# Products over 448 rows: six 128-row matmuls and a pair of 64-row halves, or seven pairs of 64-row halves

## The chip, the core and the metric

The kernel runs on one NeuronCore of a Trainium2 chip. The core has five engines with instruction streams of their own: PE (TensorE, matmuls), DVE (VectorE), ACT (ScalarE), POOL (GpSimd) and SP (SyncE, which here only issues DMAs). They meet through semaphores. The metric is the device time of one execution in microseconds (us), median of several runs; less is better.

## What is computed

x is 2048 x 448 in bf16. It is normalised row by row, and two branches are added to it: a linear attention with 16 heads of 28 columns, and a feed-forward layer with 1792 hidden columns. Cut to what matters:

```python
xn = _layernorm(x)                                    # 2048 x 448
q, k, v = split(xn @ wqkv)                            # 16 heads, Dh = 28
pq, pk = q @ w_phi, k @ w_phi                         # per head, 28 x 28
phi_q = concat(softmax(pq), softmax(-pq)); phi_k = concat(softmax(pk), softmax(-pk))
kv, z = phi_k^T v, sum(phi_k)
o = (phi_q kv) / (phi_q z + 1e-6)
h = xn @ w1 + b1;  act = h * tanh(softplus(h))        # Mish, F = 1792
out = x + o @ wo + act @ w2
```

## The kernel before

The 2048 tokens are 16 tiles of 128, taken as 8 pairs `u`, the two tiles of a pair being `par` 0 and 1. The weights of w_phi are first multiplied into those of q and k (steps `wtk`, `wmk`, `wmq`), so q, k and v are one product each. All products with 448 rows of contraction share one layout: 448 = 3 x 128 + 64. Each pair has a transposed copy `xnT[:, u]` of seven 128-row chunks: three for `par` 0, three for `par` 1, and one shared chunk whose upper 64 rows are the last 64 of `par` 0 and whose lower 64 rows are those of `par` 1 (`xchunk`).

Such a product is two steps on PE. Part **F** has six matmuls over all 128 rows, three for each `par`. Part **H** has two matmuls over 64 rows, one in the upper half of the array for `par` 0 and one in the lower half for `par` 1. Both parts of one product add into a pair of neighbouring PSUM banks, one bank for each `par`; `take2` and `free2` keep four such pairs. The part that comes second closes the sum, and ACT or DVE reads it. `pair_part` (its matmuls are line 426) does this for `v{u}`, `k{u}`, `q{u}` (448 columns, 8 pairs each) and for `f{q}.{fc}`, the first feed-forward layer (512 columns, 28 products). `wo` (line 831) does it for the output projection, whose bank also takes the second layer `g{t}` (`ffn2`, line 815, 14 matmuls over 128 rows each). `finish` (line 780) adds x and a store follows.

Three other groups of matmuls are not changed: `kv{u}` (line 641, two column halves of the array side by side), `nd{t}` (line 715, 16 small matmuls in the two 64-row halves, 60 columns each) and the transposes and weight products at the start (lines 499, 550, 574). `z12` (line 371) are twelve matmuls on zeros ahead of all others.

The order of everything is written out by hand in `ORDER`: a list of step names, each of which appends instructions to the streams of its engines. Each engine works its own stream strictly in that order; `Program.op` finds which earlier operations of other engines an operation must wait for, `resolve` drops the waits that are implied, `emit` writes them. Operations on the same PSUM bank by the same engine need no wait in this scheme. SP's stream holds nearly all DMAs: loads (`l...s`), transposes by DMA of the normalised rows (`xt{u}m`, line 511), of the query features (`e{t}`, line 681), of the attention output (`ot{u}m`, line 749), and stores (`sto`, `stt`). Steps named later: `pw`, `zero`, `pv`, `pm`, `pi` are POOL's first memsets and masks; `qd` (line 284) completes the transposed q weights on DVE, which `wmq0` and `wmq1` on PE (line 574) read; `st{u}` are row statistics on DVE; `l1ms` loads three quarters of w1 (line 271), `l2s` w2, `los` wo.

Of the kernel before, what the change touches and what calls it, by code (L numbers as in the profile page):

```python
# [38 lines left out]
class Program:  # L39
# [113 lines left out]
e9 f0.2H kn2.0 e13 f0.2F kn7.0 f0.0F f1.2F f0.1F f0.0H f0.1H f1.3H q5H kn1.0 f1.3F kn0.1 e8 q0F q0H f0.3H kn0.0 q7H  # L153
kn3.1 e5 e1 q5F q7F f0.3F f1.7F kv7 kn1.1 kv0 kv4 kv6 kv3 kv2 kv1 e0 kv5 e10 f1.1H kvz f1.7H f1.8H f1.1F f1.8F f0.6F
e14 e11 f1.5H f0.6H nd2 f0.10F f1.5F nd1 f0.10H f0.5H f0.5F f1.11F nd3 ot1m f1.11H nd0 f0.13H f0.13F e15 f1.12F f1.0F
f1.0H ot0m f1.12H los wob nd6 f1.13F f0.7F f1.10H f0.7H nd7 l2s ot3m f1.13H f1.10F f0.4F f0.4H nd5 f0.12H f0.9H f0.9F
f0.12F nd4 f0.11H f0.8H f0.8F f0.11F f1.4F f1.6H f1.4H nd10 ot2m f1.9H f1.9F f1.6F wo3F wo3H nd11 nd13 nd12 ot5m ot6m
# [10 lines left out]
def _kernel(es, nc, A_x, A_wqkv, A_w_phi, A_wo, B_w1, B_b1, B_w2, out):  # L168
# [218 lines left out]
    def take2(hold=True):  # L387
        free = [b for b in (0, 2, 4, 6) if b not in held]
        assert free, "no pair of banks"
        b = min(free, key=lambda b: max(used[b], used[b + 1]))  # L390
        touch(b, b + 1)
        if hold:
            held.add(b)
        return b
# [7 lines left out]
        touch(b)  # L402
        return b

    def pe(fn, r, w, tag):
        return op("PE", fn, r=r, w=w, tag=tag)

    open_ = {}

    def pair_part(key, part, works, r, then):
        if key not in open_:
            open_[key] = take2()
            first = True
        else:
            first = False
        b = open_[key]  # L420

        def f(e):
            for o, par, lhs, rhs in works(b):
                for c in range(3) if part == "F" else (3,):
                    k = (0, P) if part == "F" else HALF[par]
                    ins = e.matmul(o, lhs(c, k), rhs(c, k), start=first and c in (0, 3), stop=not first and c in (2, 3))  # L426
            return ins
# [168 lines left out]
        return c if c == 3 or par == 0 else 4 + c  # L596

    def tok_works(u, W):
        return lambda b: [(bank(b + par)[:, 0:D], par,
                           lambda c, k, par=par: xnT[k[0]:k[1], u, xchunk(c, par), :],  # L600
                           lambda c, k: W[k[0]:k[1], c, :]) for par in range(2)]

# [59 lines left out]


    def feat_works(W, cols, q, rows):
        return lambda b: [(bank(b + par)[0:rows, :], par,
                           lambda c, k: W[k[0]:k[1], c, cols],
                           lambda c, k, par=par: xnT[k[0]:k[1], 4 * q:4 * q + 4, xchunk(c, par), :])
                          for par in range(2)]
# [95 lines left out]
        return CUT if t == LAST else D  # L764

    out_bank = {}
    done = {t: 0 for t in range(NT)}

    def out_part(t):

        u = t // 2
        if u not in out_bank:
            out_bank[u] = take2()
        done[t] += 1
        return out_bank[u] + t % 2, done[t] == 1, done[t] == 3

    def finish(t):
        b = out_bank[t // 2] + t % 2
        n = width(t)
        op("DVE", lambda e: e.tensor_tensor(x_all[:, t, 0:n], bank(b)[:, 0:n], x_all[:, t, 0:n], ALU.add),  # L780
           r=[pb(b), ("x", t)], w=[("out", t)], tag=f"fin{t}")
        if t == LAST:
            last_columns(t, b ^ 1)
        if done[t] == done[t ^ 1] == 3:
            free2(out_bank[t // 2])

    def last_columns(t, b):
        assert done[t ^ 1] == 3
# [12 lines left out]
        op("DVE", lambda e: e.tensor_tensor(x_all[:, t, CUT:D], to, x_all[:, t, CUT:D], ALU.add), r=[pb(b), ("x", t)],  # L801
           w=[("outl", t)], tag=f"finl{t}")
# [18 lines left out]

    def wo(u, part):
        places = [out_part(2 * u + par) for par in range(2)]

        def f(e):
            for par, (b, first, last) in enumerate(places):
                for c in range(3) if part == "F" else (3,):
                    lo, hi = (0, P) if part == "F" else HALF[par]
                    cc = xchunk(c, par)
                    n = width(2 * u + par)  # L830
                    ins = e.matmul(bank(b)[:, 0:n], oT_of(u)[lo:hi, cc * P:(cc + 1) * P], Wo[lo:hi, cc, 0:n],  # L831
                                   start=first and c in (0, 3), stop=last and c in (2, 3))
            return ins
        pe(f, [("oT", u)] + [("Wo", n) for n in range(4)], [pb(b) for b, _, _ in places], f"wo{u}{part}")
        for par, (b, first, last) in enumerate(places):
            if last:
                finish(2 * u + par)
# [15 lines left out]
    for u in range(NU):  # L853
# [8 lines left out]
            add(f"xt{u}{c}", xT, u, eng)  # L862
            add(f"ot{u}{c}", oT, u, eng)
        for eng, c in (("ACT", "a"), ("DVE", "d")):
            for part in "FH":
                add(f"v{u}{part}{c}", v_mm, u, part, eng)
        for part in "FH":
# [15 lines left out]
            for which, n in ((0, "q"), (1, "k")):  # L883
                add(f"wm{n}{h}{c}", w_mm, which, h, eng)
    for q in range(2):
        for part in "FH":
            for fc in range(FC):
                add(f"f{q}.{fc}{part}", ffn1, q, fc, part)
    add("kvz", kvz)
# [75 lines left out]
```

## Time and profile before

| | |
|---|---|
| time, median of 3 runs | 153.92 us (153.82 to 154.27) |
| profiled execution: span from first to last instruction | 151.8 us |
| PE busy / weight loads busy | 147.1 us (97%), 1181 matmuls / 72.7 us (48%) |
| DVE / ACT / POOL busy | 101.2 us / 75.2 us / 40.0 us |
| granted TensorE clock, mean | 0.998 |
| DMA traffic | 17.17 MB, mean 113 GB/s |

The profile gives one execution. Its span runs from the first to the last instruction; the time of a run is taken from outside and holds 2.1 us more (153.92 - 151.8). In the timeline a row gives start, duration, engine, line, operation, out<-in, the size of the part of the array used (rows*columns), the shape and a count; consecutive instructions of one kind are merged, so a row of `x8` may hold six 128-row matmuls and two 64-row ones, under the shape of the first. Because matmuls are pipelined, their durations overlap: the distance from one start to the next tells what PE gives to each, the duration tells when its result is there. `PEld` are the weight loads, one for each matmul. Square brackets give idle time ahead of the row and what ended it; "issue" means nothing that the profile shows.

### The profile page before, as it was taken

The page shows a single profiled execution, that of the slowest core. Times are in us where ns is not written, and L with a number is a line of the kernel's source. Part 1 is how long each engine was busy: PE and PEld are TensorE (multiplying, and loading weights), DVE is VectorE, ACT ScalarE, POOL GpSimd, SP SyncE. Part 2 cuts the span into 40 slices and gives each one's busy share as a digit, 9 for nine tenths or more (in the row PEclk, how much of TensorE's full clock was granted, in tenths as well). Part 3 has the DMA queues.
Part 4 walks back from the last instruction along what each step waited for, and adds up shares of the span by engine and source line. Part 5 has one row for each costly group of instructions (what it writes and reads, how often), then busy time and mean ns, then how long its engine had stood idle before and what let it go on. Part 6 is the DMA issues. An engine that isn't in the chain of part 4 may idle for free.

```text
span 151.8 us, 2885 instructions
## 1 busy us (share of the span) xinstructions
PE 147.1 (97%) x1181; PEld 72.7 (48%) x1181; DVE 101.2 (67%) x227; ACT 75.2 (50%) x91; POOL 40.0 (26%) x58
## 2 busy tenths in 40 slices
PE   7799999999999999999999999999999999999993
PEld 2365444454444475444444444655555555455552
DVE  0699997999999203298999847798795970311221
ACT  4988999898998996756558567000000000000000
POOL 7452562499999950000000000000000000000000
PEclk9999999999999999999999999999999999999999
DMA  5994995989767091910389950030207021110302
GB/s 135 253 269 84 292 163 103 185 255 231 159 139 139 0 176 41 170 36 0 73 157 317 319 81 10 0 67 18 43 0 213 33 39 21 60 35 0 121 0 91
DMA packets 39961, 17.17 MB, mean 113 GB/s; under 512 B 33932, under 2 KB 39180, under 8 KB 39948
## 3 DMA queue, kind: packets, MB, share of 16 engines
q1 hardware_dynamic: 39776, 16.89, 50.0%
q8 instruction: 9, 0.15, 0.4%
q10 hardware_dynamic: 172, 0.10, 0.2%
q14 instruction: 4, 0.03, 0.1%
HBM read 7.02 MB, written 1.84 MB: 58 GB/s over the span
## 4 chain that ended last, share of the span: by engine, by line
PE 92%; ACT 2%; DMA 2%; DVE 1%; issue 1%
PE PS L426 51%; PE PS L815 28%; PE PS L831 7%; PE PS L715 3%; PE PS L641 2%; DMA x_all<-in_A_x_dram 2%; PE PS L574 1%; ACT junk L447 1%; DVE xn L491 1%; ACT junk L452 1%; PE PS L499 0%; DVE x_all L780 0%; ACT rmean L450 0%; ACT lnv L470 0%; ACT rstd L472 0%
## 5 line engine op out<-in xcount | busy, mean ns | idle before, releaser
L426 PE MATMUL PS<-xnT,W 128*128 128x512 bf16 (+1 forms) x224 | 46.3, 380 | 0.0
L815 PE MATMUL PS<-W,actT 128*128 128x448 bf16 (+1 forms) x224 | 42.8, 351 | 0.0
L692 ACT ACTIVATE actT<-PS,b1T 128x1024 bf16<-128x1024 f32 x28 | 30.5, 1113 | 13.7 <-PE PS L426 13.6
L815 PEld LDWEIGHTS PS<-W,actT 128*128 128x128 bf16 x224 | 21.8, 98 | 20.2 <-issue 0.4
L426 PEld LDWEIGHTS PS<-xnT,W 128*128 128x128 bf16 (+1 forms) x224 | 17.6, 97 | 23.8 <-issue 5.3
L624 POOL TENSOR_TENSOR actT<-actT,rSk 128x896 bf16<-128x896 bf16 x16 | 26.6, 1700 | 4.4 <-DVE rSk L622 4.4
L780 DVE TENSOR_TENSOR x_all<-PS,x_all 128x448 bf16<-128x448 f32 (+1 forms) x16 | 9.6, 617 | 20.9 <-PE PS L815 17.7
L620 DVE TENSOR_REDUCE Sk<-actT 128x32 f32<-128x896 bf16 x16 | 16.7, 1041 | 0.9 <-ACT actT L612 0.9
L612 ACT ACTIVATE actT<-PS 128x896 bf16<-128x896 f32 x16 | 13.7, 940 | 0.4 <-PE PS L426 0.4
L426 PE MATMUL PS<-Wpq,xnT 128*128 128x448 bf16 (+1 forms) x64 | 12.9, 352 | 0.0
L426 PE MATMUL PS<-Wpk,xnT 128*128 128x448 bf16 (+1 forms) x64 | 12.7, 353 | 0.0
L426 PE MATMUL PS<-Wkv,xnT 128*128 128x448 bf16 (+1 forms) x64 | 12.6, 353 | 0.0
L730 DVE COPY Sq<-PS 128x16 f32<-128x16 f32 x32 | 4.0, 167 | 10.8 <-PE PS L715 10.8
L456 DVE BATCH_NORM_STATS2 stats<-x_all 128x6 f32<-128x448 bf16 x14 | 8.5, 605 | 3.4 <-DMA x_all<-in_A_x_dram 3.4
L738 DVE TENSOR_TENSOR v_all<-v_all 128x464 f32<-128x464 f32 x16 | 10.3, 642 | 0.6
L734 DVE TENSOR_TENSOR v_all<-PS,Sq 128x464 f32<-128x464 f32 x16 | 10.3, 641 | 0.5
L741 DVE TENSOR_TENSOR xn<-v_all,rden 128x448 bf16<-128x448 f32 x16 | 10.0, 625 | 0.6
L736 DVE TENSOR_TENSOR v_all<-PS,Sq 128x464 f32<-128x464 f32 x16 | 10.1, 629 | 0.0
L673 ACT ACTIVATE actT<-PS 128x896 bf16<-128x896 f32 x10 | 8.5, 932 | 0.1
L426 PEld LDWEIGHTS PS<-Wpk,xnT 128*128 128x128 bf16 (+1 forms) x64 | 5.3, 97 | 6.1 <-issue 1.9
L426 PEld LDWEIGHTS PS<-Wpq,xnT 128*128 128x128 bf16 (+1 forms) x64 | 5.3, 97 | 5.7 <-issue 1.1
L426 PEld LDWEIGHTS PS<-Wkv,xnT 128*128 128x128 bf16 (+1 forms) x64 | 5.1, 97 | 5.7 <-issue 1.5
(86 smaller groups left out, 117.4 us busy)
## 6 DMA issues: line engine op xcount, KB each, us to landing
W<-in_B_w_dram SPq DMA_DIRECT2D x1, 1568.0 KB, 8.3
out_dram<-x_all SPq DMA_DIRECT2D x7, 224.0 KB, 2.2
W<-in_B_w_dram SPq DMA_DIRECT2D x1, 1344.0 KB, 7.1
x_all<-in_A_x_dram SPq DMA_DIRECT2D x4, 224.0 KB, 3.1
x_all<-in_A_x_dram SPq DMA_DIRECT2D x2, 448.0 KB, 4.8
Wkv<-in_A_wqkv_dram SPq DMA_DIRECT2D x2, 336.0 KB, 4.7
Wo<-in_A_wo_dram SPq DMA_DIRECT2D x2, 336.0 KB, 3.8
W<-in_B_w_dram SPq DMA_DIRECT2D x2, 224.0 KB, 4.4
```

The source lines that it names most:

```text
L426: ins = e.matmul(o, lhs(c, k), rhs(c, k), start=first and c in (0, 3), stop=not first and c in (2, 3))
L612: op("ACT", lambda e, s=s: e.activation(E_of(u)[:, s, :, :], two(b, D), ACT.Exp, scale=1.0 if s == 0 else -1.0), r=[pb(b), pb(b + 1)], w=[ ...
L620: op("DVE", lambda e: e.tensor_reduce(Sk[u][:, s, :], Eh(), AX.X, ALU.add), r=[("E", u, s)], w=[("Sk", u, s)], tag=f"Sk{u}.{s}")
L624: op("POOL", lambda e: e.tensor_tensor(Eh(), Eh(), ap_on(rSk[u][:, s, 0:1], [[1, 2 * H], [0, DH]]), ALU.mult), r=[("E", u, s), ("rSk", u, ...
L692: op("ACT", lambda e: e.activation(actT[:, fc, q * 1024:(q + 1) * 1024], bank(b, 2), ACT.Mish, bias=b1T[:, fc:fc + 1]), r=[("b1T",), pb(b) ...
L734: op("DVE", lambda e: e.tensor_tensor(tv(t1[i]), num(0), sx(1), ALU.mult), r=[pb(b), pb(b + 1), ("Sq", i, 1)], w=[("t1", i)], tag=f"ta{t}")
L736: op("DVE", lambda e: e.tensor_tensor(tv(t2), num(1), sx(0), ALU.mult), r=[pb(b), pb(b + 1), ("Sq", i, 0)], w=[("t2",)], tag=f"tb{t}")
L738: op("DVE", lambda e: e.tensor_tensor(t1[i], t1[i], t2, ALU.add), r=[("t1", i), ("t2",)], w=[("t1", i)], tag=f"tc{t}")
L741: op("DVE", lambda e: e.tensor_tensor(o_sb[(t // 2) % 2][:, t % 2, :].rearrange("p (h d) -> p h d", d=DH), t1[i][:, :, 0:DH], ap_on(rden[i ...
L780: op("DVE", lambda e: e.tensor_tensor(x_all[:, t, 0:n], bank(b)[:, 0:n], x_all[:, t, 0:n], ALU.add), r=[pb(b), ("x", t)], w=[("out", t)], ...
L815: ins = e.matmul(bank(b)[:, 0:width(t)], actT[:, fc, tok(t)], W2[:, fc, 0:width(t)], start=first and fc == 0, stop=last and fc == FC - 1)
L831: ins = e.matmul(bank(b)[:, 0:n], oT_of(u)[lo:hi, cc * P:(cc + 1) * P], Wo[lo:hi, cc, 0:n], start=first and c in (0, 3), stop=last and c i ...
```

## The change

Each product over 448 rows may now be cut in three parts instead of two. **A** has the three 128-row chunks of each `par` in their halves: for each chunk, the upper 64 rows of `par` 0 in the upper half of the array and the lower 64 rows of `par` 1 in the lower half, six matmuls in three pairs. **B** has the other halves, crossed over: lower rows of `par` 0, upper rows of `par` 1, again six in three pairs. **H** is as before. So a product has 14 matmuls in 7 pairs, not 8 (6 and a pair). In A and H the upper half of the array writes the bank of `par` 0, in B that of `par` 1. Where two steps on the same pair of banks differ in this, the second gets a wait on PE's own semaphore for the first (`side`, `after`). Part F remains possible, but the new `ORDER` uses A, B and H everywhere: 1541 matmuls instead of 1181, and 68 waits of PE on its own semaphore instead of none. `ORDER` is new throughout; its steps are the same but for the parts. The diff, cut to what matters:

```diff
-    def op(self, eng, fn, r=(), w=(), dma=False, tag=""):
+    def op(self, eng, fn, r=(), w=(), dma=False, tag="", after=()):
...
-        deps = []
+        deps = list(after)
...
-table lx2s lba zero lx3s pv st2b pw lkms lps pi pm st3b rs3a lkts z12 b1 pp rs2p lx1s xn2d xn3d wtk0b xt2b wtk1b lvms
-lx4s lqT2 st1 bd pk lqT0 xt3a wmk0b lqT1 rs1a wmk1a xn1d st5 rs5p v2Fd lqT3 v3Fa v3Ha k2H v2Ha k3H qd xt1m lx0s st4
-k2F rs4p wmq0d xn4d xn5p wmq1a k3F v1Fd st0 q3F k1H q3H lx6s st6 v1Hd q2H q2F rs6p st7 k1F q1F l1ts rs0p xt4m xt5m
-xn6d k4F rs7p k4H e6 v5Hd xn0d xt6m xn7d kn4.1 q1H k5H xt0m v5Fd k5F kn5.0 v6Fd kn5.1 k6F k0H xt7m ep e7 v6Ha k7H
-l1ms k6H k7F kn6.0 k0F kn6.1 e3 q6F e2 v0Fa kn2.1 kn7.1 v4Fd v0Ha v4Hd kn4.0 q6H v7Hd kn3.0 v7Fa q4F e4 e12 f1.2H q4H
...
+table lx2s pw lba zero pv pm st2b lx3s lkms lps st3b lkts z12 pi rs2p rs3a lx1s b1 xn2d wtk0b lvms lx4s xn3d xt2b
+wtk1b bd wmk0b st1 xt3a v2Ad st5 wmk1a pk lqT2 v3Ha lqT0 rs1a lqT1 v2Ha v3Aa lqT3 pp v2Bd qd xn1d k2H v3Ba lx0s k2A
+rs5p wmq0d wmq1a k2B k3A k3H q2B st4 rs4p k3B lx6s xt1m xn5p q3A q2A q2H st7 k1B rs7p st6 l1ts q3B xt5m xn4d rs6p xn7d
+kn3.0 q1B q3H k1A xt4m xt7m v1Bd k1H q1A v1Ad xn6d k5B v1Hd q1H k5A k5H st0 v5Hd rs0p v5Ad kn1.0 xt6m k4B v5Bd k7A
+l1ms kn5.0 k4A v7Hd k4H k7H v7Aa k7B v6Ad xn0d v7Ba k6H kn5.1 v6Ha k6A v6Bd e3 kn2.0 kn7.1 xt0m q4B k6B e2 v4Bd q4A
+q4H kn1.1 v4Hd v4Ad k0A kn6.0 kn3.1 v0Ba k0B e7 v0Aa e6 k0H v0Ha q6H q6A f1.2B q6B f0.0H f1.2A f0.2B kn2.1 f1.2H e4
...
+    open_ = {}
+    side = {}
+
+    def passes(part):
+        if part == "F":
+            return [(c, par, (0, P)) for par in range(2) for c in range(3)]
+        x = int(part == "B")
+        return [(c, r ^ x, HALF[r]) for c in ((3,) if part == "H" else range(3)) for r in range(2)]
+
+    def pe_pass(fn, r, b, part, tag):
+        o = pe(fn, r, [pb(b), pb(b + 1)], tag, after=[side[b, "A" if part == "B" else "B"]] if part in "ABH" and
+               (b, "A" if part == "B" else "B") in side else [])
+        side[b, "B" if part == "B" else "A"] = o
+
+    def run(e, todo, works, first, last):
+        at = {par: [n for n, x in enumerate(todo) if x[1] == par] for par in range(2)}
+        for n, (c, par, k) in enumerate(todo):
+            o, lhs, rhs = works[par]
+            ins = e.matmul(o, lhs(c, k), rhs(c, k), start=first and n == at[par][0], stop=last and n == at[par][-1])
+        return ins
...
     def pair_part(key, part, works, r, then):
+        todo = passes(part)
         if key not in open_:
-            open_[key] = take2()
...
-        pe(f, r, [pb(b), pb(b + 1)], key + part)
-        if not first:
+            open_[key] = [take2(), set()]
+        b, done = open_[key]
+        first = not done
+        done.add(part)
+        last = done in ({"F", "H"}, {"A", "B", "H"})
+        pe_pass(lambda e: run(e, todo, works(b), first, last), r, b, part, key + part)
+        if last:
             then(b)
             free2(b)
```

`wo` is changed in the same way (it calls `passes` and `pe_pass`), and `finish` counts four parts instead of three for each output tile. In the new `ORDER` the steps `kv` stand in one block as before, the `nd` steps stand among the products, and the `g` steps stand in three blocks and at the end.

More of the change, by code (lines that the diff above doesn't have):

```diff
@@ L153 @@
[L153 to L157, printed above, removed]
@@ new lines @@
+f1.6A f0.12H f0.9B los e10 f1.11H f1.6H e15 e14 f0.9A f0.13B f0.9H l2s f0.13A f0.13H f1.13A nd0 f1.11B f1.13H f1.11A
+f0.6A f1.13B f0.6B nd3 f1.7A f0.6H f1.7H f0.4B f1.7B nd2 f0.4H f0.4A e1 f0.7B f0.5H f0.7H ot1m f0.7A f1.10A f0.5A
+f1.4B nd7 f0.5B f1.10B f1.4H f1.10H f1.4A f0.3B nd1 f0.3H f0.11H f0.11A f1.8H f0.3A f1.5A f0.11B f1.5B f1.8B ot0m
+f1.5H f0.10B nd5 f1.8A f0.10H f0.10A f0.8B f1.9B nd4 f0.8A f0.8H f1.9H f1.9A wo1B ot2m nd6 wo1H ot3m nd13 wo1A nd12 g2
+g0 g3 g1 nd11 ot6m f1.12B f1.0A f1.12H f1.0B wo0H wo0A f1.0H wo0B wo2A wo2H sto0 f1.12A wo6H nd9 sto1 wo6A wo2B wo6B
@@ L160 @@
+nd10 nd8 ot4m g5 g12 ot5m g4 g11 g9 g10 g13 wo4H nd14 wo4B wo3A wo5H wo3H wo5A nd15 ot7m wo3B g6 sto6 g7 g8 sto3 wob
+wo5B wo7B wo4A wo7A sto2 wo7H sto5 g14 sto4 g15 stt14 stt15
 """
@@ L403, in take1, with pe @@
         return b
-    def pe(fn, r, w, tag):
-        return op("PE", fn, r=r, w=w, tag=tag)
+    def pe(fn, r, w, tag, after=()):
+        return op("PE", fn, r=r, w=w, tag=tag, after=after)
     open_ = {}
+    side = {}
[14 more added lines that the diff above has]
+        return ins
     def pair_part(key, part, works, r, then):
+        todo = passes(part)
         if key not in open_:
-            open_[key] = take2()
[L417 to L427, printed above, removed]
-        pe(f, r, [pb(b), pb(b + 1)], key + part)
-        if not first:
+            open_[key] = [take2(), set()]
[5 more added lines that the diff above has]
+        if last:
             then(b)
@@ L598, in tok_works @@
     def tok_works(u, W):
-        return lambda b: [(bank(b + par)[:, 0:D], par,
+        return lambda b: [(bank(b + par)[:, 0:D],
                            lambda c, k, par=par: xnT[k[0]:k[1], u, xchunk(c, par), :],
@@ L664, in feat_works @@
     def feat_works(W, cols, q, rows):
-        return lambda b: [(bank(b + par)[0:rows, :], par,
+        return lambda b: [(bank(b + par)[0:rows, :],
                            lambda c, k: W[k[0]:k[1], c, cols],
@@ L766, in _kernel, with parts_of @@
     out_bank = {}
+    STEPS = ORDER.split()
+    def parts_of(t):
+        return 3 if f"wo{t // 2}F" in STEPS else 4
     done = {t: 0 for t in range(NT)}
@@ L774, in out_part @@
         done[t] += 1
-        return out_bank[u] + t % 2, done[t] == 1, done[t] == 3
+        return out_bank[u] + t % 2, done[t] == 1, done[t] == parts_of(t)
     def finish(t):
@@ L783, in finish @@
             last_columns(t, b ^ 1)
-        if done[t] == done[t ^ 1] == 3:
+        if done[t] == done[t ^ 1] == parts_of(t):
             free2(out_bank[t // 2])
     def last_columns(t, b):
-        assert done[t ^ 1] == 3
+        assert done[t ^ 1] == parts_of(t)
         to = bank(b)[:, D:D + 64]
@@ L823, in wo @@
         places = [out_part(2 * u + par) for par in range(2)]
+        todo = passes(part)
         def f(e):
[L826 to L832, printed above, removed]
+            at = {par: [n for n, x in enumerate(todo) if x[1] == par] for par in range(2)}
+            for n, (c, par, (lo, hi)) in enumerate(todo):
+                b, first, last = places[par]
+                cc = xchunk(c, par)
+                w = width(2 * u + par)
+                ins = e.matmul(bank(b)[:, 0:w], oT_of(u)[lo:hi, cc * P:(cc + 1) * P], Wo[lo:hi, cc, 0:w],
+                               start=first and n == at[par][0], stop=last and n == at[par][-1])
             return ins
-        pe(f, [("oT", u)] + [("Wo", n) for n in range(4)], [pb(b) for b, _, _ in places], f"wo{u}{part}")
+        pe_pass(f, [("oT", u)] + [("Wo", n) for n in range(4)], places[0][0], part, f"wo{u}{part}")
         for par, (b, first, last) in enumerate(places):
@@ L864, in _kernel @@
         for eng, c in (("ACT", "a"), ("DVE", "d")):
-            for part in "FH":
+            for part in "FABH":
                 add(f"v{u}{part}{c}", v_mm, u, part, eng)
-        for part in "FH":
+        for part in "FABH":
             add(f"k{u}{part}", k_mm, u, part)
@@ L885, in _kernel @@
     for q in range(2):
-        for part in "FH":
+        for part in "FABH":
             for fc in range(FC):
```

4 lines of the change are left out of this document (2 added, 2 removed).

## Prediction

> **What bounds the kernel now.** I read the page's busy table first, then the slices and the chain that ended last, then the table of waits.
>
> ```profile
> PE 147.1 (97%) x1181; PEld 72.7 (48%) x1181; DVE 101.2 (67%) x227; ACT 75.2 (50%) x91; POOL 40.0 (26%) x58
> ...
> PE   7799999999999999999999999999999999999993
> ...
> PEclk9999999999999999999999999999999999999999
> ...
> PE 92%; ACT 2%; DMA 2%; DVE 1%; issue 1%
> ```
> ```profile
> PEld PS L426 <- issue: 9.8, 26, 0.4
> ```
>
> PE is busy in every slice after the first and carries 92% of the chain, at the full clock. It waits for almost nobody, so time can only come from what PE does between its matmuls, or be lost by making PE wait. The waits row shows where to look: the weight loads of the products stood still 26 times, about 0.4 us each, for no releaser. The PE timeline shows what these places are.
>
> ```profile
> 22.91 1.59 PE L426 MATMUL PS<-Wpk,xnT 128*128 128x448 bf16 x8
> 24.34 0.35 PE L426 MATMUL PS<-Wkv,xnT 64*128 64x448 bf16 x2
> 24.53 0.35 PE L426 MATMUL PS<-Wpq,xnT 64*128 64x448 bf16 x2
> 24.72 0.35 PE L426 MATMUL PS<-Wpk,xnT 64*128 64x448 bf16 x2
> 25.00 1.31 PE L426 MATMUL PS<-Wkv,xnT 128*128 128x448 bf16 x6
> 26.15 1.30 PE L426 MATMUL PS<-Wpk,xnT 128*128 128x448 bf16 x6
> 27.29 1.30 PE L426 MATMUL PS<-Wkv,xnT 128*128 128x448 bf16 x6
> 28.42 1.59 PE L426 MATMUL PS<-Wpk,xnT 128*128 128x448 bf16 x8
> ```
>
> Twelve 128-row matmuls start from 26.15 to 28.42: 0.189 us each. A pair of 64-row halves follows the one before it after 0.19 (24.34, 24.53, 24.72). So two halves side by side cost what one full matmul costs, and the 14 matmuls of the new product in 7 pairs cost what 6 and a pair cost now. The changes between the two shapes cost extra. From 22.91 to 24.34 lie six full matmuls and a pair, 7 x 0.189 = 1.32, and it took 1.43: 0.11 to go in. From 24.72 to 25.00 lies one pair, 0.28 for 0.19: 0.09 to come out.
>
> **The change, part by part.** *Changes of shape.* Counted along PE's stream, before goes 20 times from 128-row matmuls into 64-row ones and 21 times back; `nd` counts as 64-row. After, it does this 6 and 6 times (the start's weight products, four blocks of `g`), and once more comes out into `kv`, which before was entered from full matmuls. That removes 14 x 0.11 + 15 x 0.09 = **2.9 us** of PE time, nothing of which lay beside another wait of PE. I take the same price for the 512-column products.
>
> The Trainium skill, "TensorEngine Tiling (Array Packing)", Key Properties, says that changing the tiling mode, not just the tile, drains TensorE. The rows agree and give the drain's size.
>
> *The waits of PE on itself.* 68 of them, each behind a step that used the same banks the other way round. Behind a waiting step stands all of PE's later stream, and for that ACT's exponentials. The trace has no such wait; the nearest rows are a wait of ACT for a pair, and one of PE for DVE.
>
> ```profile
> 12.26 0.10 PEld L426 LDWEIGHTS PS<-Wkv,xnT 64*128 64x128 bf16 x2 [0.37 <-issue]
> ...
> 12.67 1.73 ACT L504 ACTIVATE v_all<-PS 128x896 bf16<-128x896 f32 x2 [0.38 <-PE PS L426]
> ```
> ```profile
> 6.27 2.18 DVE L491 TENSOR_SCALAR xn<-x_all,mv,rstd 128x448 bf16<-128x448 bf16 x6 [0.47 <-POOL rstd L467]
> ...
> 8.50 0.56 PE L499 MATMUL PS<-ident,xn 128*128 128x128 bf16 x7 [0.19 <-DVE xn L491]
> ```
>
> ACT starts 0.41 us after the pair that it needs; PE starts 0.05 after DVE's end at 8.45. So a step that waits for a pair can start some 0.42 us after that pair's start. With one pair between the two, its turn would come after 2 x 0.19 = 0.38, and it loses 0.04; I take 0.03, as two 512-column passes last longer and cover more. With two or more between, 0.57 and up, it loses nothing. In the new order 11 waits have one pair between (or one `nd`, 0.22 by a row below), 57 have more, none has less. That is 11 x 0.03 = **0.3 us**. Bounds: nothing, and 68 times the price of a change of shape, 68 x 0.11 = 7.5 us. I take the value by the wake-up rows, which are of the same kind.
>
> *The start.* `pw` now stands ahead of `zero` on POOL.
>
> ```profile
> 0.80 0.10 POOL L314 MEMSET zeros<- 128x2 bf16 x1 [0.29 <-POOLq L950]
> ...
> 1.21 0.58 POOL L334 MEMSET Wbd<- 112x512 bf16 x1
> ```
> ```profile
> 0.95 4.53 PE L371 MATMUL PS<-zeros 128*128 128x512 bf16 x12 [0.95 <-POOL zeros L314]
> 5.41 0.18 PE L686 MATMUL PS<-ident,b_rows 14*128 14x14 bf16 x1
> 6.65 0.65 PE L550 MATMUL PS<-ident,Wkv 128*112 128x128 bf16 x8 [1.06 <-DMA Wkv<-in_A_wqkv_dram]
> ```
>
> The matmuls on zeros start 0.5 later and the bias step ends near 6.1. PE waits there for a load until 6.65 in either kernel, so this costs nothing. Without that cover it would cost 0.5. Next, `v2A` is put between the two halves of the k weights' product; it fills places where PE now waits for DVE (0.19 at 8.50 above, 0.19 at 9.49 below). But `wmq0` comes earlier on PE and still needs `qd`.
>
> ```profile
> 9.49 0.41 PEld L574 LDWEIGHTS PS<-Wbd,Eq 112*128 112x128 bf16 x8 [0.19 <-DVE Eq L506]
> ```
> ```profile
> 13.89 0.23 DVE L284 COPY WqT<-WqT 128x256 bf16<-128x256 bf16 x1
> ...
> 14.17 0.90 PEld L574 LDWEIGHTS PS<-Wbd,WqT 112*128 112x128 bf16 x16 [0.17 <-DVE WqT L284]
> ```
>
> Before, PE does 22 passes between the k weights' product and `wmq0`; after, 18. Four passes, 0.76, are put behind `wmq0`, so PE is there near 13.5 instead of 14.2. `qd` stands behind four statistics and the copy of `v2` on DVE, and I see no reason for it to end before 13.6 or after the 14.1 of now (13.89 + 0.23). PE then waits 0.1 to 0.6 us. Of the two waits of 0.19 a part returns, as `v2A` and the `v3H` after it now wait for the v weights' landing and for ACT's copy of `xt3`. The start costs -0.2 to +0.5, and I take **+0.2**.
>
> *SP's queue.* `l1ms` is moved ahead of `xt0m` and three `e` steps; before, it stands behind all six `xt`.
>
> ```profile
> 23.88 3.90 SPq L511 DMA_TRANSPOSE xnT<-xn  x3
> 27.83 1.31 SPq L681 DMA_TRANSPOSE EqT<-Eq  x1
> 29.18 0.59 SPq L271 DMA_DIRECT2D W<-in_B_w_dram  x1
> ```
> ```profile
> 32.07 6.43 SPq L681 DMA_TRANSPOSE EqT<-actT  x2
> ```
> ```profile
> W<-in_B_w_dram SPq DMA_DIRECT2D x1, 1344.0 KB, 7.1
> ...
> xnT<-xn SPq DMA_TRANSPOSE x6, 3.1
> ```
>
> A transpose takes 1.3 us to issue and lands 3.1 after its start, so 1.8 after its issue ends. The load lands 7.1 after its issue, at 36.3. The transpose issued behind it at 32.07 and the next one together held the queue 6.43 us, to 38.50; less the second one's 1.3, the first was stuck until about 37.2, 0.9 after the load's landing. In the new order one `xt` and two `e` fewer stand ahead of the load: issue near 29.2 - 3 x 1.3 = 25.3, landing 32.4. `xt0m` is then the second transpose behind it, stuck until 33.3, landed at 35.1. Its first reader, `k0A`, comes 108 passes after `wmq1`: `wmq0` near 13.8, 0.9 for the 16 matmuls of `wmq0` and `wmq1` (the 0.90 above), and 108 x 0.19 make 35.2. So there is no margin; if it lands as I sum, it costs 0 to 0.3, and I take **0.2**. Bounds: nothing, and 2.4 us if two more issues of 1.2 are in its way. The same order holds for `l2s` and `ot1m`, but there the load starts earlier than before (`los` and `l2s` follow `kv` closely) and I count nothing.
>
> The tail, `g14`, `g15` and the last store, is as before, and PE is the last bound there. DVE and ACT do the same operations.
>
> The sum: -2.9 + 0.3 + 0.2 + 0.2 = **-2.2 us**. Against the profiled execution the span goes from 151.8 to 149.6; the 2.1 us outside it stay, and the median of 153.9 goes to **151.7 us**.
>
> **The rivals.** *A wait of PE on itself empties PE as a change of shape does.* Then the place of the loss is every `after`, 68 x 0.11 = 7.5 us instead of 0.3, and the time is 151.7 + 7.2 = 158.9, slower. It decides from 0.037 us for each wait on (2.5 / 68). For it: a wait stops the weight loads that run ahead. Against: waits of PE that are long satisfied stand all over before's stream; by the program's semaphores the products at 27.29 and 28.42 begin with one on ACT, and their distances are 0.19 as elsewhere. Chance 0.06.
>
> *Each matmul costs a slot of its own.* The new products issue 360 more matmuls. The nearest price is that of `nd`, which is all slots and hardly any columns.
>
> ```profile
> 95.32 0.66 PE PS L715 x48
> ```
>
> That is 0.0138 us each; 360 x 0.0138 = 5.0 us, and the time would be 151.7 + 5.0 = 156.7. Against it: three pairs in a row at 24.34 to 24.72 show no such cost, as both halves start together. Chance 0.03. The Trainium skill, "TensorEngine Tiling (Array Packing)", Instruction Overhead, has about 60 cycles for every matmul, which speaks against cutting matmuls in two; by the rows it is hidden behind the columns of the other half.
>
> *The transposes come late.* `xt0m` lands 1 to 2.4 us after its place, by one more stuck issue, or another transpose with little margin does (`ot1m` behind `l2s`). Then PE stands still for 1 to 2.4 us, or up to 3.5 where both places are hit, instead of 0.2: 152.5 to 155.0, most likely 153.3. For it: the margin is near zero by my sum. Against: ACT and `take2` leave PE other steps only in the written order, so nothing hides it, but a single place is concerned. Chance 0.15.
>
> That the changes of shape do not go away can be excluded: they are in PE's stream as counted.
>
> **How the numbers follow.** The measurement of this kernel can tell about 0.3%, 0.46 us. The forecast (150.9 to 152.6: each small term from its near end to about twice its value) has 0.76. The late transposes have 0.15, a third of it each for faster (up to 153.4), same (to 154.4) and slower. The two rivals above have 0.09, slower. So faster 0.76 + 0.05 = 0.81, same 0.05, slower 0.14. The range takes in the forecast and the late transposes with one place hit: 150.9 to 154.1.
>
> **What would show it.** Right: in the timeline, `A`, `B` and `H` rows run on at 0.19 (448 columns) with no 0.3 gaps, the weight loads' idle for "issue" at the products falls from 26 places to about 8, and PE's last matmul ends about 2.2 us earlier. Wrong: idle of PE or PEld with PE itself as releaser of 0.1 or more each; distances over 0.20 between pairs inside one part; PE waiting for `xnT` by DMA near 35 us or for DVE near 13.8 by more than 0.6.

## The result, and the profile after

The changed kernel is slower: 155.23 us median (154.67 to 155.62, 4 runs) against 154.01 (153.82 to 154.27, 4 runs), ratio 1.0073 with a 95% interval of 1.0049 to 1.0098. The profiled execution took 155.41 us, its span 153.4 against 151.8, with the clock at 1.00. The prediction was 151.7, faster: it was wrong, and the time lies above its range. (Ratios here are formed from undisturbed runs alone, so a ratio need not be that of the two medians.)

The page of the changed kernel: busy times, PE's slices, and the shares of the chain that ended last.

```profile
PE 145.5 (95%) x1541; PEld 74.4 (48%) x1541; DVE 105.3 (69%) x229; ACT 73.3 (48%) x89; POOL 40.1 (26%) x58
...
PE   6898998999899999999988999999999999999993
...
PE 71%; DVE 17%; DMA 6%; POOL 2%; issue 1%; ACT 1%; DVEq 0%; POOLq 0%
```

PE's share of the chain has fallen from 92% to 71%, and DVE's has risen from 1% to 17%. A slice is 3.8 us: the 8s in PE's row at 12 to 15, 23 to 27, 38 to 42 and 77 to 84 us are new. And DVE is busy 4.1 us longer (105.3 for 101.2) with two instructions more. These two are copies of v out of PSUM that ACT made before: those of pairs 2 and 6, where the closing step was `v2Ha` and `v6Ha` and is now `v2Bd` and `v6Bd`. DVE's copies of v before, and after:

```profile
L506 DVE CAST v_all<-PS 128x896 bf16<-128x896 f32 x3 | 3.1, 1038 | 0.0
```
```profile
L522 DVE CAST v_all<-PS 128x896 bf16<-128x896 f32 x5 | 5.2, 1043 | 0.0
```

So 2.1 us of DVE's work is new. The page alone suggests that PE got its gain and then waited for DVE.

**The gain is there.** PE's timeline in a stretch without outside waits:

```profile
28.12 1.30 PE L433 MATMUL PS<-Wpk,xnT 64*128 64x448 bf16 x12
29.26 0.35 PE L433 MATMUL PS<-Wkv,xnT 64*128 64x448 bf16 x2
29.45 0.54 PE L433 MATMUL PS<-Wpk,xnT 64*128 64x448 bf16 x4
29.82 0.73 PE L433 MATMUL PS<-Wkv,xnT 64*128 64x448 bf16 x6
30.39 0.73 PE L433 MATMUL PS<-Wpk,xnT 64*128 64x448 bf16 x6
```

Six pairs of halves take 1.14 (28.12 to 29.26), so 0.19 a pair, as one full matmul did. The last row, `k7B`, waits on PE itself for `k7H` in the row of `x4`, with `v7A` between; it starts 0.57 after `v7A`, exactly three passes. The waits of the weight loads show the rest:

```profile
PEld PS L433 <- PE PS L433: 2.4, 7, 0.3
...
PEld PS L433 <- issue: 0.5, 2, 0.3
```

Of the 26 places of 0.4 us at the products two are left. PE itself appears as a releaser of weight loads only. The prediction named such idle time of 0.1 or more as a sign that it is wrong, and seven places show it; but the matmuls behind them keep their distance, so they cost nothing.

**The loss is PE standing still.** All rows of PE's timeline with idle time ahead of them, but for the zeros:

```profile
8.01 0.56 PE L515 MATMUL PS<-ident,xn 128*128 128x128 bf16 x7 [0.97 <-DVE xn L507]
14.41 0.96 PE L590 MATMUL PS<-Wbd,WqT 112*128 112x112 bf16 x16 [0.45 <-DVE WqT L287]
23.92 0.74 PE L433 MATMUL PS<-Wpk,xnT 64*128 64x448 bf16 x6 [0.31 <-DMA xnT<-xn]
26.98 0.74 PE L433 MATMUL PS<-Wpk,xnT 64*128 64x448 bf16 x6 [0.42 <-DVE v_all L522]
37.36 0.74 PE L433 MATMUL PS<-Wpk,xnT 64*128 64x448 bf16 x6 [0.37 <-DMA xnT<-xn]
40.57 0.93 PE L433 MATMUL PS<-Wpq,xnT 64*128 64x448 bf16 x8 [0.39 <-ACT actT L689]
80.78 0.40 PE L731 MATMUL PS<-KVZ,EqT 56*128 56x60 bf16 x16 [0.66 <-DMA EqT<-Eq]
83.50 3.63 PE L433 MATMUL PS<-xnT,W 64*128 64x512 bf16 x32 [0.39 <-DVE v_all L752]
```

The bracket shows idle time only after the pipelined matmul ahead has ended, so it understates. From start to start, less the steady distance of the pass ahead, the eight cost 1.13, 0.51, 0.47, 0.58, 0.54, 0.55, 0.82 and 0.55, and one of 0.20 at 41.53 comes with them: 5.35 us. By the same measure the waits of before cost 1.12 at 6.65, 0.35 at 8.50 and 0.20 at 9.49, 1.67 in all, none of it after 10 us. The books close:

```profile
6.11 0.18 PE L702 MATMUL PS<-ident,b_rows 14*128 14x14 bf16 x1
...
150.42 0.57 PE L818 MATMUL PS<-W,actT 128*128 128x64 bf16 x14
```
```profile
148.75 0.57 PE L797 MATMUL PS<-W,actT 128*128 128x64 bf16 x14
```

The last group of matmuls starts 1.67 later than before (second fence: before). The bias step starts 0.70 later (6.11 for 5.41), waits cost 3.7 more (5.35 - 1.67), and what is left, 1.67 - 0.70 - 3.68 = -2.7, is PE's own work. So the gain of 2.9 came in nearly whole, and 4.4 us were lost beside it: 0.67 up to `wmq0` (0.70 by the bias step, and waits of 1.13 + 0.51 for 1.67 before), and 3.71 behind it.

**Who is late.** The chain, from DVE to the wait at 37.36:

```profile
31.72 0.35 DVE rSk L638
32.07 2.10 DVE xn L507 x3
...
34.20 3.02 DMA xnT<-xn
...
37.36 1.32 PE PS L433 x12
```

The normalisation of pair 0 (`xn0d`, three instructions of line 507) ends at 34.17; its transpose, `xt0m`, is issued at once at 34.20. It did not stand in SP's queue at all: the load of w1 was issued at 27.40, and one transpose behind it from 28.04 to 29.28. DVE is late. Its rows, beside POOL's:

```profile
23.74 1.90 DVE L507 TENSOR_SCALAR xn<-x_all,mv,rstd 128x448 bf16<-128x448 bf16 x2
...
23.74 2.18 DVE L507 TENSOR_SCALAR xn<-x_all,mv,rstd 128x448 bf16<-128x448 bf16 x3
...
31.99 2.18 DVE L507 TENSOR_SCALAR xn<-x_all,mv,rstd 128x448 bf16<-128x448 bf16 x3
```
```profile
23.90 1.70 POOL L640 TENSOR_TENSOR actT<-actT,rSk 128x896 bf16<-128x896 bf16 x1 [1.39 <-DVE rSk L638]
...
32.15 1.70 POOL L640 TENSOR_TENSOR actT<-actT,rSk 128x896 bf16<-128x896 bf16 x1 [0.62 <-DVE rSk L638]
```
```profile
22.99 2.46 DVE L491 TENSOR_SCALAR xn<-x_all,mv,rstd 128x448 bf16<-128x448 bf16 x9
```

Before (third fence), nine such instructions take 2.46, 0.8 for three, and they are over at 25.5, ahead of POOL's first multiplication at 27.92. In the new order `kn3.0` stands ahead of `xn6d`, and `kn5.0` ahead of `xn0d`. Their multiplications start on POOL 0.16 us into the normalisation, and three instructions take 2.18. The first row shows how: the second instruction, 64 columns, is over at 23.74 + 1.90 = 25.64, 0.04 after POOL's multiplication (23.90 + 1.70 = 25.60). In the second meeting the same instruction lasts from 32.20 to 33.88, and POOL's from 32.15 to 33.85. So it looks held until POOL is done, and not merely slowed down; `pool_later` below tries it.

The Trainium skill, "SBUF — State Buffer", Who interferes with whom, says just this: VectorE and GpSimd share one pair of ports, a VectorE `tensor_scalar` in a two-port mode needs it, whoever starts first has it for the whole instruction, and the other blocks fully. The rows agree, with 1.3 us for each of the two meetings; that these instructions ran in such a mode, no row says.

### The profile page after: what moved, and what is told of

Read it like the earlier page. It is cut to its first block, busy times and chain, and to the rows that moved or that the text cites. A ratio compares the mean times of both kernels' runs of the same rounds, so it can differ in the third digit from the quotient of the medians.

```text
span 153.4 us, 3609 instructions
## 1 busy us (share of the span) xinstructions
PE 145.5 (95%) x1541; PEld 74.4 (48%) x1541; DVE 105.3 (69%) x229; ACT 73.3 (48%) x89; POOL 40.1 (26%) x58
## 4 chain that ended last, share of the span: by engine, by line
PE 71%; DVE 17%; DMA 6%; POOL 2%; issue 1%; ACT 1%; DVEq 0%; POOLq 0%
PE PS L433 29%; PE PS L836 28%; PE PS L853 7%; DVE xn L507 5%; DMA Wkv<-xn 4%; PE PS L374 3%; DVE stats L472 3%; PE PS L657 2%; PE PS L731 2%; DMA xnT<-xn 2%; DVE Sk L636 2%; DVE v_all L522 2%; POOL xn L502 1%; ACT actT L689 1%; DVE mv L474 1%
## 5 line engine op out<-in xcount | busy, mean ns | idle before, releaser
L433 PE MATMUL PS<-xnT,W 64*128 64x512 bf16 x392 | 45.3, 376 | 0.4 <-DVE v_all L752 0.4
L433 PEld LDWEIGHTS PS<-xnT,W 64*128 64x128 bf16 x392 | 17.8, 94 | 22.5 <-PE PS L433 2.4
L433 PE MATMUL PS<-Wpk,xnT 64*128 64x448 bf16 x112 | 13.8, 349 | 1.1 <-DMA xnT<-xn 0.7
L433 PE MATMUL PS<-Wkv,xnT 64*128 64x448 bf16 x112 | 13.6, 349 | 0.0
L433 PE MATMUL PS<-Wpq,xnT 64*128 64x448 bf16 x112 | 12.7, 349 | 0.4 <-ACT actT L689 0.4
L507 DVE TENSOR_SCALAR xn<-x_all,mv,rstd 128x448 bf16<-128x448 bf16 (+2 forms) x21 | 9.5, 507 | 0.1
L433 PEld LDWEIGHTS PS<-Wpk,xnT 64*128 64x128 bf16 x112 | 5.3, 94 | 6.7 <-DVE v_all L522 1.6
L433 PEld LDWEIGHTS PS<-Wpq,xnT 64*128 64x128 bf16 x112 | 5.4, 94 | 6.1 <-ACT actT L689 0.8
```

Of the source, the lines that this page charges most:

```text
L433: ins = e.matmul(o, lhs(c, k), rhs(c, k), start=first and n == at[par][0], stop=last and n == at[par][-1])
L507: op("DVE", lambda e, t=t, lo=lo, hi=hi, at=at: e.tensor_scalar(X[:, at:at + hi - lo], x_all[:, t, lo:hi], mv[:, t, 0:1], rstd[:, t:t + 1] ...
```

## The experiments

**Theory A**: the halves give what was forecast, and the new order takes it back: on DVE, where a normalisation meets a multiplication on POOL or stands behind steps of `kn`, and on SP, where transposes stand behind the load of w2. **Rival B**: the halves cost it themselves, by the waits on PE or the number of matmuls. **Rival C**: only w1's load on SP matters. All shifts below are changes of `ORDER` unless code is shown.

### POOL's two multiplications wait for DVE (`pool_later`)

```diff
-        op("POOL", lambda e: e.tensor_tensor(Eh(), Eh(), ap_on(rSk[u][:, s, 0:1], ...
+        if (u, s) in LATER:
+            return
+        k_mult(u, s)
...
+    LATER = {(3, 0), (5, 0)}
...
-xn6d
+xn6d km3.0
...
-xn0d
+xn0d km5.0
```

`km` issues the multiplication with a wait for DVE's last operation.

> The changed kernel, with one thing altered: POOL's two multiplications phik3.0 and phik5.0, which in the changed kernel run from 23.90 to 25.60 and from 32.15 to 33.85, wait until DVE has finished the normalisation of pair 6 and of pair 0. DVE's and PE's streams are the same. Theory A (the time is lost in the new order, and a good part of it where a normalisation on DVE meets a multiplication on POOL): the two rows of 2.18 us for three L507 instructions fall to about 0.9, all of DVE behind them is 1.3 us earlier at the first place and up to 2.6 at the second, the waits of PE at 26.98, 37.36, 40.57 and 41.53 (0.58, 0.54, 0.55, 0.20) shrink or go: 1.0 to 1.9 us less than the changed kernel, 153.3 to 154.2. Rival B (the halves, their waits on PE itself or their number, cost it): the rows change, the time stays at 155.2. Rival C (only the load W1 on SP's queue ahead of the transposes): no more than 0.3 less.

Measured: 153.87 us median (152.06 to 155.55, 10 runs), ratio 0.9926 (0.9879 to 0.9974). DVE and PE in its timeline:

```profile
23.35 0.80 DVE L507 TENSOR_SCALAR xn<-x_all,mv,rstd 128x448 bf16<-128x448 bf16 x3
...
30.66 0.79 DVE L507 TENSOR_SCALAR xn<-x_all,mv,rstd 128x448 bf16<-128x448 bf16 x3
```
```profile
23.53 0.74 PE L433 MATMUL PS<-Wpk,xnT 64*128 64x448 bf16 x6 [0.31 <-DMA xnT<-xn]
```

Nothing is changed but when POOL runs, and 2.18 becomes 0.80. Between 22 and 43 us PE waits once, for pair 5, whose normalisation was never on DVE; the waits at 26.98, 37.36, 40.57 and 41.53, 1.87 us together, are gone. By the medians the kernel is 1.36 faster than the changed one, as theory A expected, though its ten runs spread over 3.5 us and three of them reach the changed kernel's 155. B and C, which allowed no gain and at most 0.3, fall for this part of the loss: PE's stream and SP's order were not touched.

### The three kn steps behind the normalisations (`kn_behind_xn`)

```diff
-kn3.0 q1B q3H k1A xt4m xt7m v1Bd k1H q1A v1Ad xn6d
+q1B q3H k1A xt4m xt7m v1Bd k1H q1A v1Ad xn6d kn3.0
...
-kn1.0 xt6m k4B v5Bd k7A l1ms kn5.0 k4A v7Hd k4H k7H v7Aa k7B v6Ad xn0d
+xt6m k4B v5Bd k7A l1ms k4A v7Hd k4H k7H v7Aa k7B v6Ad xn0d kn1.0 kn5.0
```

> The changed kernel with three steps moved: kn3.0 behind xn6d, and kn1.0 and kn5.0 behind xn0d. So DVE does the normalisations first, and POOL has no multiplication beside them. Theory A: both L507 rows of 2.18 fall to 0.9, and pair 0 is normalised some 5 us earlier (2 x 1.3 and two steps of 1.4); PE's waits at 26.98, 37.36, 40.57, 41.53, 1.9 us together, go nearly all: 153.2 to 153.9. If the order on DVE counts and the meeting with POOL doesn't, this kernel gains and the one with POOL's waits alone doesn't. Rival B: 155.2.

Measured: 154.18 us (152.99 to 154.71, 10 runs), ratio 0.9985 (0.9954 to 1.0016): 1.05 below the changed kernel, less than the 153.2 to 153.9 expected and no better than POOL's wait alone. The rows of line 507 are short again and the four waits gone, but in its profile two others are longer, 0.73 from start to start at 24.56 (pair 5's transpose) and 1.29 at 82.19. To place the normalisations earlier than they need be gives nothing more.

### POOL's start as before (`start_as_before`)

```diff
-pw lba zero pv pm
+lba zero pv pw pm
```

> The changed kernel with POOL's first steps in the order of the kernel before: zero, pv, pw instead of pw, zero, pv. The prediction said that pw ahead of zero costs nothing, as PE waits for a load until 6.65 anyway: then 155.2, within 0.2. Theory A (b1, b1T and with them DVE's first normalisation start 0.5 later and PE stands 1.13 at 8.01 for it): 0.1 to 0.6 less than the changed kernel, 154.6 to 155.1, and the wait at 8.01 is 0.4 to 1.0.

Measured: 155.51 us (154.00 to 156.34, 10 runs), ratio 1.0043 (1.0001 to 1.0084). No gain that can be told from the changed kernel's 1.0073, and none of 0.5 that could be excluded: the intervals overlap. The profiled execution, the fastest of the ten, did change at the place. PE waits for the load until 6.60 as the prediction said, and then 0.50 for DVE at 7.59, where the changed kernel lost 1.13 at 8.01; `wmq0` starts at 13.96 for 14.41. So the prediction's claim that `pw` ahead of `zero` costs nothing is neither shown nor refuted by the times, and its reason does not hold in the changed kernel's trace: there PE stands for DVE's first normalisation, which stands behind the bias step (6.11, 6.32 and 6.41 in the rows of PE and DVE) and so behind the matmuls on zeros.

### The load of w2 later (`l2s_later`)

```diff
-f1.6H e15 e14 f0.9A f0.13B f0.9H l2s
+f1.6H e15 e14 f0.9A f0.13B f0.9H
...
-f0.5H f0.7H ot1m
+f0.5H f0.7H ot1m l2s
```

In the changed kernel the transpose `e1` behind the load holds the queue for 5.31 us, `ot1m` is issued at 75.88, and DVE waits 1.88 for its landing:

```profile
69.89 0.59 SPq L301 DMA_DIRECT2D W<-in_B_w_dram  x1
70.53 5.31 SPq L697 DMA_TRANSPOSE EqT<-Eq  x1
75.88 21.90 SPq L765 DMA_TRANSPOSE Wkv<-xn  x4
```
```profile
81.44 0.62 DVE L757 TENSOR_TENSOR xn<-v_all,rden 128x448 bf16<-128x448 f32 x1 [1.88 <-DMA Wkv<-xn]
```

> The changed kernel with one step moved: the load of w2 (l2s) behind ot1m on SP, so that e1 and ot1m no longer stand behind the load in the queue. If the transposes stuck behind that load make PE's waits at 80.78 (0.82) and 83.50 (0.55), they go: 0.8 to 1.4 us less than the changed kernel, 153.8 to 154.4. If DVE's chain of the nd steps makes them, nothing changes: 155.2.

Measured: 154.55 us (153.99 to 155.18, 10 runs), ratio 1.0028 (1.0009 to 1.0048), 0.7 below the changed kernel. SP and DVE:

```profile
69.67 1.72 SPq L697 DMA_TRANSPOSE EqT<-Eq  x1
76.41 1.22 SPq L765 DMA_TRANSPOSE Wkv<-xn  x1
77.68 0.58 SPq L301 DMA_DIRECT2D W<-in_B_w_dram  x1
```
```profile
81.14 0.63 DVE L757 TENSOR_TENSOR xn<-v_all,rden 128x448 bf16<-128x448 f32 x1 [1.05 <-DMA Wkv<-xn]
```

`e1` goes out in 1.72 and the wait of `nd` at 80.78 is gone. But `ot1m`, issued 1.3 ahead of the load, landed only 4.6 us later (76.41 to 81.0), where `xt0m` above took 3.02, so DVE waits still, and PE behind it (0.38 at 83.21). The lower end of what was expected was 0.8. The load seems to delay a transpose in front of it too; no run here tries that by itself.

### Halves alone, and the order alone

The two halves of the change, each without the other. In the first, every step that is no part of a product stands as before the change (the lines are against the kernel before):

```diff
-xn1d st5 rs5p v2Fd lqT3 v3Fa v3Ha k2H v2Ha k3H qd xt1m lx0s st4 k2F rs4p wmq0d
+v2Bd v3Ba xn1d st5 v2Aa rs5p v3Aa v2Ha lqT3 qd xt1m k2H lx0s k2A v3Ha k3H k2B st4 k3A rs4p wmq0d
...
```

> Halves alone: the products in parts A, B and H as in the changed kernel, but every step that is not a part of a product (loads, transposes, normalisations, kn, nd, kv, g, stores) in the order of the kernel before; only the parts are spread among themselves so that at least one pass lies between two parts that use the banks the other way round (1 to 18 passes, 60 waits of PE on itself). Theory A: the changes of shape fall from 41 to 12, some 2.9 us of PE time, and DVE, POOL and SP keep the order of before, so the gain is there: 150.5 to 152.0. Rival B (waits on itself, or the number of matmuls, cost it): no faster than before, 154 to 157.

Measured: 153.18 us (152.42 to 153.86, 10 runs), ratio 0.9919 (0.9890 to 0.9949). Faster than before, so B falls a second time; 1.0 us and not the 2 to 3.5 expected. In its trace, with this spreading of the parts, PE waits for pair 4:

```profile
22.71 1.88 PE L433 MATMUL PS<-Wpk,xnT 64*128 64x448 bf16 x18 [0.94 <-DMA xnT<-xn]
```

In the second, the other steps stand as in the changed kernel, and the products are parts F and H:

```diff
-v2Ad st5 wmk1a pk lqT2 v3Ha lqT0 rs1a lqT1 v2Ha v3Aa lqT3 pp v2Bd qd xn1d k2H v3Ba lx0s k2A
+st5 v2Ha wmk1a pk v3Fa lqT2 lqT0 rs1a k2H lqT1 v3Ha lqT3 pp qd xn1d v2Fd lx0s
...
```

> The new order alone: every step that is not a part of a product stands as in the changed kernel, and the products are parts F and H as in the kernel before, with no wait of PE on itself; 57 changes of shape against 41 before and 16 in the changed kernel. Theory A: the order's losses are nearly all there, and the changes of shape on top, (57 - 16) x 0.1 = 4.1 us more PE time than in the changed kernel, of which a part falls into PE's waits: 156.5 to 159. Rival B (halves cost more than they gain): faster than the changed kernel, below 155.

Measured: 158.24 us (157.13 to 158.53, 4 runs), ratio 1.0233 (1.0176 to 1.0290): 3.0 above the changed kernel, 4.1 us of changes of shape less what falls into PE's waits. DVE's busy time sorts the four kernels; first the halves alone, then the order alone:

```profile
PE 145.2 (96%) x1541; PEld 75.6 (50%) x1541; DVE 101.4 (67%) x227; ACT 74.9 (50%) x91; POOL 39.8 (26%) x58
```
```profile
PE 149.3 (96%) x1181; PEld 72.1 (46%) x1181; DVE 105.1 (68%) x229; ACT 73.8 (48%) x89; POOL 40.3 (26%) x58
```

101.2 and 101.4 in the old order, 105.3 and 105.1 in the new one, whatever the parts. DVE's 4 us belong to the order: 2.1 are the two copies of v, which the new order gives to DVE with either kind of parts, and 2.7 went with the two meetings in `pool_later` (102.6 there); the rest of DVE's rows is a little shorter.

### A wait on PE itself with no pass between (`no_pass_between`)

```diff
-q6A f1.2B q6B f0.0H f1.2A f0.2B kn2.1 f1.2H e4 f0.2A kn4.0 f0.2H
+q6A q6B kn2.1 f1.2A f1.2H f1.2B e4 kn4.0 f0.2A f0.2H f0.2B
...
```

> The changed kernel with parts A, H and B of each product of the first feed-forward layer directly behind one another (28 products), at the place of the last of them: 29 waits of PE on itself with no pass between instead of 0, everything else in the same order. By the prediction's wake-up rows such a wait costs 0.42 - 0.19 = 0.23, 28 x 0.23 = 6.4 us for the products of the feed-forward layer, less what falls into PE's other waits (1.4 us there): 160 to 162. If a wait on itself costs nothing at any distance: 155 to 156.

Measured: 160.95 us (160.59 to 161.20, 4 runs), ratio 1.0420 (1.0373 to 1.0467). The weight loads:

```profile
PEld PS L433 <- PE PS L433: 16.4, 30, 0.6
```
```profile
61.80 1.19 PEld L433 LDWEIGHTS PS<-xnT,W 64*128 64x128 bf16 x14 [0.56 <-PE PS L433]
63.55 1.19 PEld L433 LDWEIGHTS PS<-xnT,W 64*128 64x128 bf16 x14 [0.56 <-PE PS L433]
```

One product takes 1.75 (61.80 to 63.55) where its seven passes need 7 x 0.216 = 1.51: 0.24 for its wait, where 0.23 was worked out ahead from the wake-up of ACT. 28 x 0.23 = 6.4 us, of which 5.7 show. With one pass or more between, as the change has it, such idle time is left in the weight loads, but the products keep their distance.

### Versions that combine (`combo1`, `halves_old_order_2`, `best_a`, `best_b`)

`combo1` is the changed kernel with POOL's start, `qd`, `l2s` and, as above, the three `kn` steps moved:

```diff
-pw lba zero pv pm
+lba zero pv pw pm
...
-lqT3 pp v2Bd qd xn1d
+lqT3 qd pp v2Bd xn1d
...
-q7H q0B e12 q7A
+q7H q0B e12 l2s q7A
...
```

> The changed kernel with five steps or groups moved: POOL's start as before (zero, pv, pw), kn3.0 behind xn6d and kn1.0, kn5.0 behind xn0d, qd ahead of the copy of v2 on DVE, l2s behind e12, where SP has nothing to do for 8 us. Theory A: with PE's waits of 0.5 at 14.41, 1.9 us between 26 and 42 and 1.4 at 80 to 84 gone, of 4.0 us in all: 151.3 to 153.0. Rival B: 155.2.

Measured: 153.59 us (153.00 to 154.46, 10 runs), ratio 0.9950 (0.9919 to 0.9981): faster than before, but not the 151.3 to 153.0 expected. Behind 10 us three waits of PE for others stay:

```profile
23.79 0.74 PE L433 MATMUL PS<-Wpk,xnT 64*128 64x448 bf16 x6 [0.71 <-DMA xnT<-xn]
36.65 0.74 PE L433 MATMUL PS<-Wpk,xnT 64*128 64x448 bf16 x6 [0.39 <-DMA xnT<-xn]
...
81.82 3.41 PE L433 MATMUL PS<-xnT,W 64*128 64x512 bf16 x30 [0.51 <-DVE v_all L752]
```

The second of them is the prediction's own fear come true. Here DVE is early, and `xt0m` goes to SP at 29.81; but it is the second transpose behind the load of w1 (issued at 25.68), and SP holds it for 4.53 us, where the changed kernel took 1.22:

```profile
29.81 4.53 SPq L527 DMA_TRANSPOSE xnT<-xn  x1
```

So with DVE out of the way the queue is the limit at this place.

`halves_old_order_2` moves `k4B`, and `k4A` with it, in the halves alone:

```diff
-q2B k4B xt5m xn6d k1A k4A q1B rs7p e6 v5Ad k4H
+q2B xt5m xn6d k1A q1B k4B rs7p e6 v5Ad k4A k4H
```

> As halves alone in the old order, with one step moved: k4B, which there waited 1.10 us at 22.71 for the transposed rows of pair 4, comes behind q1B and v5A ahead of k4A, 9 passes later. Theory A: the wait falls to below 0.3 and the time by up to 0.8 to 1.1: 152.1 to 152.9. If the rows come late enough to hold the later steps too, the wait only moves: 153.2.

Measured: 153.03 us (152.46 to 154.01, 10 runs), ratio 0.9939 (0.9912 to 0.9965). The wait at 22.7 is 0.15, but 0.3 and more have come at 16.91, 28.22 and 42.45: it moved. The expectation failed, its alternative came.

`best_a` and `best_b` start from this one; from `wmk1a` on each step is placed anew, by the durations of the traces, with three conditions: no normalisation on DVE beside a multiplication on POOL, room for transposes around the two big loads, a pass or more ahead of each wait of PE on itself. The middle of `best_b`:

```diff
...
+xn0d k1A k4B q1H ep xt5m q1A k4A k4H xn7d q1B v5Ad kn2.1 k5B xt6m e6 v5Bd k5A v5Hd v6Ha xt0m k5H
...
```

> The halves in an order worked out anew from the old one: up to wmk1a (near 10 us) as in the kernel before, behind it every step placed so that no normalisation on DVE runs beside a multiplication of POOL, l1ms and l2s stand on SP where the next transposes have room, and no part of a product that uses the banks the other way round follows with less than one pass between (12 changes of shape). Theory A: PE stands still only some 2 us at the start, as before, and runs 2.9 us less: 151.0 to 152.3. If something that the traces do not show (the number of matmuls or of waits) costs more than the changes of shape give, 153 or more.

> A second such order, found from the same start, with w1's load and the transposes of pairs 6 and 7 placed otherwise on SP. Expected as for the first: 151.0 to 152.5; a difference between the two of over 0.5 comes from the transposes' landing.

Measured: `best_a` 152.42 us (151.74 to 152.83, 4 runs), ratio 0.9890 (0.9858 to 0.9922); `best_b` 151.87 us (151.50 to 153.07, 4 runs), ratio 0.9872 (0.9827 to 0.9917). The page and PE's timeline of `best_b`:

```profile
PE 145.5 (97%) x1541; PEld 76.6 (51%) x1541; DVE 101.2 (67%) x227; ACT 74.7 (50%) x91; POOL 40.1 (27%) x58
...
PE 90%; DMA 3%; ACT 2%; SPq 2%; DVE 0%; issue 0%
```
```profile
17.35 0.74 PE L433 MATMUL PS<-Wkv,xnT 64*128 64x448 bf16 x6 [0.58 <-ACT Wpq L520]
```

`best_a` lies just above the 151.0 to 152.3 expected, `best_b` within its range; in the trace of `best_a` PE stands 1.03 at 17.60 for a transpose, which `best_b` has not. DVE is back at 101.2 in `best_b`, PE carries 90% of the chain, and after 10 us one row with a wait of PE is left. With the same halves this kernel beats both: 2.2 us below the 154.03 of before beside it, 3.4 below the changed one.

## Why the prediction was wrong, point by point

- **Changes of shape, -2.9: right.** PE's own time fell by 2.7, and with an order that holds the rest together the kernel gained 2.2 (`best_b`, 154.03 beside it for before).
- **Waits of PE on itself, +0.3: right in mechanism, a little too dear.** The price by the wake-up rows, 0.23 with no pass between, came out at 0.24; with one or more nothing shows.
- **The start, +0.2: too small.** `wmq0` waits 0.51 for `qd`, and 0.1 to 0.6 was given. But the bias step comes 0.70 later, and this shows: the start cost 0.67 in the profiled execution, above the 0.5 that was the upper end. 0.47 of it is the later start of the matmuls on zeros by `pw`, 0.22 their longer run in this execution (4.75 for 4.53), and the waits are as long as before. The prediction let PE wait for the load alone and left out DVE, whose first normalisation stands behind the bias step.
- **SP's queue, +0.2, with DVE at nothing: the step that failed.** All that was lost behind `wmq0` had this term of 0.2, and 3.7 us were measured. The prediction found the right place, `k0A` near 35 with no margin, and the wrong queue. It asked when SP can issue `xt0m` and took for granted that the rows to be transposed are ready. They were ready at 34.17, on DVE, by the two meetings with POOL and the `kn` steps moved ahead. The prediction wrote "DVE and ACT do the same operations" and counted nothing for them. That is not so: two copies of v went from ACT to DVE (one of them, of `v2`, the prediction itself has on DVE in its part on the start), and their order and time changed too. `pool_later` takes away 1.87 of the 3.7 in the trace, 1.4 us by the medians.
- **`l2s` and `ot1m`, counted at nothing: wrong.** That the load starts earlier was no protection. In the kernel before, `ot1m` went out at 73.18, ahead of the load at 79.81; in the new order the load goes out at 69.89, and `ot1m` behind it at 75.88. The two waits behind it cost 1.37 of the 3.7, and `l2s_later` gained 0.7 by the medians. The last 0.47, at 23.92, is pair 5: it is normalised on POOL until 20.53 and its transpose is issued at 20.56, so SP's queue is not the cause. Why POOL came a microsecond later than before (18.79 for 17.80) was not tried.
- **The rivals.** "The transposes come late" (0.15, 152.5 to 155.0) is what PE sees in three of the eight rows, and through DVE in that of 83.50, but the queue that it blamed is the cause of the late ones at 80 us only. Its 3.5 us for both places hit lie near the measured 3.7 by luck, as half of the loss came from DVE. The two rivals on PE fell: neither the waits, at their distances here, nor the slots cost anything that shows.

What stays open is how the loss splits to a tenth between its places, as the kernels of one order spread over 1 to 3.5 us from run to run. A part of this spread lies at the start. With the same steps there, the matmuls on zeros took 4.22 in the profiled execution of `pool_later` and 5.30 in that of `l2s_later`, and `wmq0` started at 14.02 and 14.94. So 0.4 of what the span of `pool_later` shows against the changed kernel (14.02 for 14.41) is luck of that execution.

## What to carry to other kernels

When an order changes, walk each engine's queue, not only that of the engine which gains and that of the DMAs: a step moved ahead on DVE delays all behind it, and what it starts on POOL can hold DVE for nearly as long as POOL's instruction lasts (1.68 of 1.70 us here). A sum that finds "no margin" at one place should ask every producer in the chain of that place. And a good local change is best tried in the old order first: here the halves gained in it at once, and the new order hid it.

## What the runs showed of the hardware

- A VectorE `tensor_scalar` on bf16 that met a GpSimd `tensor_tensor` begun ahead of it ended with that instruction, both times: 1.68 us for an instruction of 64 columns that takes 0.29 at the least. `tensor_reduce` and the copies out of PSUM ran beside POOL's multiplications in their usual 1.03 to 1.09 us.
- Behind a load of 1.5 MB the next transpose took 5.31 us to issue, and behind one of 1.3 MB the second took 4.53 (`combo1`); others take 1.2 to 1.3. One that was issued 1.3 us ahead of a load took 4.6 us to land instead of 3; this was seen once, and that the load is the cause is not shown.
- The matmuls on zeros took 4.22 to 5.30 us for the same twelve. From `pool_later`, the changed kernel and `best_b`:

```profile
1.42 4.22 PE L374 MATMUL PS<-zeros 128*128 128x512 bf16 x12 [1.42 <-POOL zeros L317]
```
```profile
1.42 4.75 PE L374 MATMUL PS<-zeros 128*128 128x512 bf16 x12 [1.42 <-POOL zeros L317]
```
```profile
0.95 5.30 PE L374 MATMUL PS<-zeros 128*128 128x512 bf16 x12 [0.95 <-POOL zeros L317]
```

In the third row all twelve start 0.43 apart. In the first the distance falls to 0.22 at 4.4 us, behind 7 of them, and in the second at some 5.4 us, behind 9, though both began at 1.42. The Trainium skill, "TensorE: Matmul & The Clock Gate", Part 1: The HAM clock gate (the "warmup" mystery), has the clock set by a free-running window of activity and not by a count of matmuls. The rows agree that no fixed count decides. They do not show that it is the clock, as the granted clock of the profile reads 1.00 in all these stretches.
